# The channel weight's load issued in two pieces of partitions

## The chip, the cores and the metric

The kernel runs on one core of one Trainium2 chip. The metric is the device time of one execution in microseconds. All times of "before" are medians or single executions of the same program; a profile is one execution recorded by the hardware profiler.

## The reference

The input is q, k and v of shape (8, 8, 576, 64), two weight tensors w_r and w_i of shape (64, 512, 512), and a channel weight w_ch of shape (512, 512), all fp32. A causal attention with a window of 64 positions is followed by a spectral mix and a channel step:

```
scores = q @ k.T / sqrt(64);  masked to 0 <= i - j < 64
x      = softmax(scores) @ v                 -> (8, 576, 512)
X      = rfft(x, axis=1)[:, :64]             64 modes, complex
Y[m]   = X[m] @ (w_r[m] + i w_i[m])          one complex 512 x 512 product per mode
u      = x + irfft(Y, n=576)
out    = u + relu(u @ w_ch)                  fp32
```

The mode weights are the bulk of the input: 127 matrices of 1 MB are read (w_i of mode 0 isn't needed). w_ch is one matrix of 1 MB.

## The kernel before

**Attention.** For each of the 8 batches k, q and v are loaded (one DMA each, converted to bf16 on the way), transposed on TensorE, and worked through in windows of 512 score columns. The result x stays in SBUF in bf16 (`x_sb`). A forward transform on TensorE (`trigF`) makes the modes' inputs `XQ`.

**Modes.** The function `mode(m)` multiplies `XQ` with the two weight tiles of mode m: 16 matmuls of 128x128 by 128x16 per tile (line 563), summed into PSUM (`psy`). Eight modes share one PSUM tile, which `keep_y` copies into `YT` or `YTl`. The modes from 60 on go through `last_mode` (line 757) in a written order with idle matmuls (lines 721 and 723) between them.

**Weights.** Every weight is one DMA of 128 partitions, issued from GpSimd (POOL) by `load_w` (line 115): in the source each partition reads 8 KB of fp32 in one run and writes 4 KB of bf16. A tile's buffer is used again as soon as its mode is done: `mode` calls `refill_w`, which issues the next load. The DMAs of POOL use eight completion semaphores in turn, so a load is issued only when the load eight places before it has landed.

**The channel weight.** Inside the loop over the modes, after mode 6, one more DMA from POOL (line 608) fills `wch`, a tile of [128, 4, 512] in fp32r: partition p holds rows p, 128 + p, 256 + p and 384 + p of w_ch, four runs of 2 KB. It is read first by `channel` (line 594), which from mode 17 on computes x @ w_ch for each tile of x, and later by `turned` (line 706), which computes Y @ w_ch.

**End.** After the last weight the remaining rows of the modes' outputs are turned; small parts of them move from SBUF to SBUF (`send`, line 845: `yw<-yl` and `Yb<-yl`, 8 partitions of 2 KB each). Then `rectify` and `finish` compute the inverse transform, the relu and the sum, and the output is stored.

**Order.** TensorE's order is written by hand in the stretches under `manual_schedule`; elsewhere a scheduler orders each engine's instructions, and POOL's DMAs in the loop over the modes are among them.

Of the kernel before, what the change touches and what calls it, by code (L numbers as in the profile page):

```python
# [20 lines left out]
def view(ap, off, dims):  # L21

    return bass.AP(ap.tensor, ap.offset + off, [list(ap.ap[0])] + [list(d) for d in dims])
# [3 lines left out]
def kernel(  # L27
# [10 lines left out]
    nc = tc.nc  # L38
# [136 lines left out]
    for i in range(4):  # L175
        half = i % 2
        pp = slice(64 * (i // 2), 64 * (i // 2) + 64)
# [78 lines left out]
    for half in range(2):  # L256
        pp = slice(64 * half, 64 * half + 64)
# [233 lines left out]
    wch = late.tile([128, NC, DM], FP32R, name="wch")  # L491
# [80 lines left out]
    with ExitStack() as p2a:  # L572
# [28 lines left out]
        for m in range(L0 * MG):  # L601
            mode(m)
            if m == 8:
                for b in range(1, B, 2):
                    tc.keep_in_program_order(nc.scalar.copy(out=x_sb[64:128, b - 1, NT - 1, :],
                                                            in_=x_sb[64:128, b, NT - 1, :]))
            if m == 6:
                nc.gpsimd.dma_start(out=wch, in_=moe_w_ch.rearrange("(c p) e -> p c e", p=128))
            if m == Z_M:
                ps_t = p2a.enter_context(tc.tile_pool(name="ps_t", bufs=2, space=PSUM, reuse_waits="tile"))  # L610
                ps_z = p2a.enter_context(tc.tile_pool(name="ps_z", bufs=2, space=PSUM, reuse_waits="tile"))
# [219 lines left out]
    with tc.manual_schedule(engines={mybir.EngineType.PE, mybir.EngineType.Activation, mybir.EngineType.DVE,  # L831
                                     mybir.EngineType.Pool, mybir.EngineType.SP}):
        nc.vector.tensor_copy(out=view(YT2, R - RL, [[NR, NC], [R, 2], [1, RL]]),
                              in_=view(psl, 0, [[RL * B, NC], [RL, 2], [1, RL]]))
# [103 lines left out]
```

## Time and profile before

| | |
|---|---|
| median of 6 runs | 430.11 us (429.16 to 431.49) |
| the profiled execution's own time | 431.29 us |
| its span, first to last instruction | 429.5 us |
| mean granted TensorE clock | 0.797 |
| busy: PE, weight loads, DVE, ACT, POOL | 329.9, 234.2, 176.9, 164.3, 97.5 us |
| DMA | 92.17 MB written to the destinations, mean 215 GB/s |
| HBM read | 162.53 MB |
| issue to landing of a mode weight, median | 19.1 us |
| issue to landing of wch | 16.5 us |

The table's times are those of one profiled execution, except for the first row. A DMA of POOL counts as busy on POOL while its descriptors are made; the transfer itself runs later on the core's 16 DMA engines, and its landing is the last of 16 completion marks. GB/s counts bytes as they are written, so that a weight that is converted from fp32 to bf16 counts half of what was read.

### The profile page before, as it was taken

To read this page: it belongs to the slowest core of one execution; us is meant where nothing else is said; L and a number is where in the kernel's file an instruction comes from. 1 tells how busy PE (TensorE), PEld (TensorE's weight loads), DVE (VectorE), ACT (ScalarE), POOL (GpSimd) and SP (SyncE) were. 2 spreads that over 40 slices of the span, in tenths; PEclk is the share of its full clock that TensorE was granted. 3 is DMA by queue.
4 is the path that set the end of the run, shared out by engine and by line. 5 is a ranking of instruction groups with operands and counts; after the bars stand their busy time and mean duration, and the time that the engine had idled before them with its cause. 6 is when DMAs were issued, how large, how long until landed. Compare 5 with 4: busy or idle time off the path is not lost.

```text
span 429.5 us, 11626 instructions
## 1 busy us (share of the span) xinstructions
PE 329.9 (77%) x5186; PEld 234.2 (55%) x5186; DVE 176.9 (41%) x372; ACT 164.3 (38%) x290; POOL 97.5 (23%) x187
## 2 busy tenths in 40 slices
PE   6989999999998986422498797896367785498992
PEld 5755765665665476411376575664244552366681
DVE  5566764666764300306333342331113332141893
ACT  4585765676774211201031232222113221131991
POOL 7131231232012141212122121121111132100610
PEclk9999996899996565555588898887557866599998
DMA  7999999999999999999999999999999999993797
GB/s 141 212 214 212 212 214 213 209 213 213 213 204 193 212 210 260 214 213 214 213 214 214 213 213 214 214 213 214 214 213 214 214 213 213 214 214 69 237 365 298
DMA packets 28882, 92.17 MB, mean 215 GB/s; under 512 B 3136, under 2 KB 3392, under 8 KB 28832
## 3 DMA queue, kind: packets, MB, share of 16 engines
q0 software_dynamic: 25920, 82.52, 96.6%
q1 hardware_dynamic: 2768, 8.78, 5.4%
q8 instruction: 40, 0.66, 0.5%
q10 hardware_dynamic: 144, 0.13, 0.1%
q14 instruction: 10, 0.08, 0.0%
HBM read 162.53 MB, written 9.44 MB: 400 GB/s over the span
## 4 chain that ended last, share of the span: by engine, by line
DMA 44%; PE 35%; issue 9%; DVE 7%; ACT 2%; POOL 0%; DVEq 0%; POOLq 0%
DMA wt<-in_moe_w_r_dram 26%; DMA wt<-in_moe_w_i_dram 18%; PE pso L316 7%; PE pst L218 6%; PE psy L563 4%; PE psv L235 3%; PE psx L338 3%; DVE x_sb L324 3%; PE pso L856 3%; PE pss L372 3%; PE pss L272 2%; PE pss L291 2%; DVE vT L59 2%; ACT vt L58 1%; DVE ot L879 1%
## 5 line engine op out<-in xcount | busy, mean ns | idle before, releaser
L563 PE MATMUL psy<-XQ,wt 128*128 128x16 bf16 x1616 | 61.0, 191 | 67.6 <-DMA wt<-in_moe_w_i_dram 32.5
L563 PEld LDWEIGHTS <-wt 128*128 128x128 bf16 x1616 | 53.0, 104 | 83.0 <-DMA wt<-in_moe_w_i_dram 37.9
L591 DVE CAST xT<-pxt 128x256 fp32r<-128x256 bf16 (+1 forms) x68 | 26.5, 435 | 59.7 <-PE pxt L584 38.0
L115 POOL DMA_DIRECT2D wt<-in_moe_w_r_dram x54 | 29.0, 536 | 89.2 <-DMA wt<-in_moe_w_r_dram 39.6
L594 PE MATMUL psz<-wch,xT 128*128 128x512 f32 x144 | 47.5, 475 | 0.0
L596 ACT CAST Z<-psz 128x512 fp32r<-128x512 f32 x36 | 21.1, 586 | 66.4 <-PE psz L594 65.3
L115 POOL DMA_DIRECT2D wt<-in_moe_w_i_dram x52 | 27.9, 536 | 79.9 <-DMA wt<-in_moe_w_i_dram 46.4
L297 ACT ACTIVATE et<-pss 128x512 bf16<-128x512 f32 x72 | 39.2, 600 | 13.8 <-PE pss L291 13.8
L316 PE MATMUL pso<-vt,et 128*64 128x65 bf16 (+1 forms) x576 | 35.1, 213 | 4.8 <-DVE x_sb L324 4.7
L316 PEld LDWEIGHTS <-et 128*64 128x64 bf16 (+1 forms) x576 | 24.5, 117 | 17.5 <-issue 10.0
L594 PEld LDWEIGHTS psz<-wch,xT 128*128 128x128 f32 x144 | 30.1, 224 | 6.2 <-ACT Z L596 0.3
L324 DVE TENSOR_TENSOR x_sb<-pso,rcp 128x640 bf16<-128x640 f32 x32 | 26.3, 823 | 0.9
L59 DVE CAST YT<-psy 128x256 fp32r<-128x256 f32 x6 | 2.5, 425 | 50.7 <-PE psy L563 50.7
L879 DVE TENSOR_TENSOR ot<-pso,x_sb 128x512 f32<-128x512 f32 x35 | 22.3, 685 | 1.8 <-PE pso L856 1.5
L59 DVE CAST x_sb<-psj 128x512 bf16<-128x512 f32 x16 | 11.0, 689 | 27.0 <-PE psj L768 26.9
L272 PE MATMUL pss<-band,ident_bf 64*64 64x512 bf16 x136 | 20.9, 428 | 1.5 <-ACT et L297 1.5
L58 ACT CAST YT<-psy 128x256 fp32r<-128x256 f32 x6 | 2.2, 373 | 51.7 <-DVE YT L59 51.7
L59 DVE COPY vT<-pst 128x768 bf16<-128x768 bf16 x16 | 15.3, 958 | 14.6 <-PE pst L218 14.6
L58 ACT CAST x_sb<-psj 128x512 bf16<-128x512 f32 x16 | 9.4, 586 | 25.9 <-PE psj L768 25.9
L861 ACT ACTIVATE pso<-pso 128x512 f32<-128x512 f32 x36 | 19.2, 588 | 0.3 <-PE pso L856 0.2
L291 PE MATMUL pss<-qT,kT 64*64 64x128 bf16 (+1 forms) x640 | 17.8, 225 | 0.2 <-issue 0.2
L58 ACT COPY qT<-pst 128x768 bf16<-128x768 bf16 x16 | 12.9, 814 | 7.8 <-PE pst L218 7.6
(163 smaller groups left out, 526.6 us busy)
## 6 DMA issues: line engine op xcount, KB each, us to landing
wt<-in_moe_w_r_dram POOLq DMA_DIRECT2D x54, 512.0 KB, 19.1
wt<-in_moe_w_i_dram POOLq DMA_DIRECT2D x52, 512.0 KB, 19.1
out_dram<-ot SPq DMA_DIRECT2D x15, 512.0 KB, 5.3
rk<-in_k_dram POOLq DMA_DIRECT2D x8, 576.0 KB, 8.7
rq<-in_q_dram POOLq DMA_DIRECT2D x8, 576.0 KB, 11.9
rv<-in_v_dram POOLq DMA_DIRECT2D x8, 576.0 KB, 10.9
wy<-in_moe_w_r_dram POOLq DMA_DIRECT2D x3, 512.0 KB, 17.4
wy<-in_moe_w_i_dram POOLq DMA_DIRECT2D x3, 512.0 KB, 19.1
```

The costliest lines, as they stand in the source:

```text
L58: return nc.scalar.copy(out=o, in_=i)
L59: return nc.vector.tensor_copy(out=o, in_=i)
L115: nc.gpsimd.dma_start(out=wt, in_=src[m].rearrange("(p c) e -> p c e", c=NC))
L272: nc.tensor.matmul(out=pss[(2 * w + hh) % 3][64 * half:64 * half + 64, :], lhsT=ident_bf[pp, pp], rhs=view(band[pp], 128 * half, [[0, WIN ...
L291: nc.tensor.matmul(out=pss[(2 * w + hh) % 3][64 * half:64 * half + 64, col:col + nq], lhsT=kTs[b % 2][pp, g, 64 * kb:64 * kb + 64], rhs=qT ...
L297: nc.scalar.activation(out=et[:, hh, :], in_=pss[(2 * w + hh) % 3], func=ACT_F.Exp, scale=EX_SCALE)
L316: nc.tensor.matmul(out=pso[po, hh, (i // 2) * VW:(i // 2) * VW + D + 1], lhsT=et[pk, hh, col:col + 64], rhs=vt[pk, 1 - f % 2, 2 * hh + g / ...
L324: nc.vector.tensor_tensor(out=view(x_sb, b * NT * DM + g * D, [[4 * D, 2], [DM, NT], [1, D]]), in0=view(pso, 0, [[512, 2], [VW, NT], [1, D]]),
L563: nc.tensor.matmul(out=psy[:, m % MG, e, :], lhsT=w[:, c, 128 * e:128 * e + 128], rhs=XQ[:, c, :, 1 - im:3 - im, m], start=(m % MG == im + ...
L591: nc.vector.tensor_copy(out=xT[:, :, w * k:w * k + w], in_=view(psts[k], j, [[128, NC], [n, w]]))
L594: nc.tensor.matmul(out=psz, lhsT=xT[:, c, :], rhs=wch[:, c, :], start=(c == 0), stop=(c == NC - 1))
L879: nc.vector.tensor_tensor(out=ot[:, j], in0=ps, in1=x_sb[:, b, t, :], op=ALU.add)
```

## The change

The load of `wch` is issued as two DMAs: partitions 0 to 7, and partitions 8 to 127. Each has the three dimensions partition, chunk (4) and column (512). The bytes are the same and lie in the same places afterwards.

```diff
             if m == 6:
-                nc.gpsimd.dma_start(out=wch, in_=moe_w_ch.rearrange("(c p) e -> p c e", p=128))
+                for pp in (slice(0, 8), slice(8, 128)):
+                    nc.gpsimd.dma_start(out=wch[pp], in_=moe_w_ch.rearrange("(c p) e -> p c e", p=128)[pp])
```

In the built program the orders of PE, DVE, ACT and SP are the same as before. On POOL the piece of 8 partitions stands where the whole load stood, two mode weights follow it, and then comes the piece of 120 partitions.

## The prediction

> **What bounds the kernel now.** I read the page's slices and queue table first. The 16 DMA engines are busy from the second slice to the last weight, at one rate.
>
> ```profile
> span 429.5 us, 11626 instructions
> ...
> DMA  7999999999999999999999999999999999993797
> GB/s 141 212 214 212 212 214 213 209 213 213 213 204 193 212 210 260 214 213 214 213 214 214 213 213 214 214 213 214 214 213 214 214 213 213 214 214 69 237 365 298
> ...
> q0 software_dynamic: 25920, 82.52, 96.6%
> ...
> q8 instruction: 40, 0.66, 0.5%
> ```
>
> The digits are 9 in slices 2 to 36, and the rate is about 213 GB/s of bytes written, of bf16 out of fp32: twice that is read. Only the slice of the channel weight (260) stands out, since that load writes fp32. Next, the order of PE at the end of that stretch, to see who waits for the last bytes:
>
> ```profile
> 390.41 0.63 PE L757 MATMUL psl<-XQ,wy 128*128 128x16 bf16 x16 [0.42 <-DMA wy<-in_moe_w_r_dram]
> 390.87 1.10 PE L721 MATMUL psd<-Z,ident_r 128*128 128x512 f32 x2
> 391.81 0.66 PE L723 MATMUL psd<-x_sb,ident_bf 128*128 128x48 bf16 x20
> 392.85 0.65 PE L757 MATMUL psl<-XQ,wy 128*128 128x16 bf16 x16 [0.38 <-DMA wy<-in_moe_w_i_dram]
> 393.33 0.66 PE L723 MATMUL psd<-x_sb,ident_bf 128*128 128x48 bf16 x20
> 394.17 1.15 PE L706 MATMUL psw<-wch,YT 128*112 128x512 f32 x4 [0.17 <-DVE YT L835]
> ```
>
> PE fills in with idle matmuls and then waits for each weight. The last one releases it at 392.85; the tail that follows takes 429.5 - 392.85 = 36.7 us. So a microsecond on the last landing is a microsecond of the kernel. Then POOL's queue around the edit:
>
> ```profile
> 155.49 0.75 POOL L608 DMA_DIRECT2D wch<-in_moe_w_ch_dram  x1 [0.63 <-PE psy L563]
> 156.23 0.54 POOL L115 DMA_DIRECT2D wt<-in_moe_w_i_dram  x1
> 159.09 0.53 POOL L115 DMA_DIRECT2D wt<-in_moe_w_r_dram  x1 [2.32 <-PE psy L563]
> 160.01 0.53 POOL L115 DMA_DIRECT2D wt<-in_moe_w_i_dram  x1 [0.40 <-PE psy L563]
> 162.85 0.53 POOL L115 DMA_DIRECT2D wt<-in_moe_w_r_dram  x1 [2.31 <-DMA wt<-in_moe_w_i_dram]
> ```
>
> and the view of the tile:
>
> ```profile
> L594 PE MATMUL psz<-wch,xT x144: 388/399/776, 212.7 to 297.8; 128*128 128x512 f32 x144
> ...
> DMA to landing us min/median/max: 16.5/16.5/16.5
> ```
>
> The load is issued at 155.49, lands at 172.0, and its first reader starts at 212.7.
>
> **Which DMA engine is late.** Every transfer leaves 16 completion marks in the trace, one per DMA engine. At wch's landing they come 0 to 0.33 us after the first for ten engines, then at 0.68, 1.00, 1.09, 1.24, 1.87 and 2.00. At the last weight eight are within 0.75 us, and the others at 2.34, 2.91, 3.10, 3.14, 3.37, 3.44, 4.06 and 4.12: the last mark is at 392.81, the first at 388.69. The steps come with the 40 instruction packets (16 KB, 0.89 to 1.09 us each): the packet at 297.29 puts the last engine from 3.03 to 4.03 us behind. At 2.45 us a weight the latest engine has never run dry. Its sum of work is the end of the stream; the others have spare time, two excepted, the one at 4.06 (0.06 us) and with more room that at 3.44.
>
> **The change, part by part.** One POOL issue becomes two. In the built program's order the scheduler puts the 8-row piece where the load was, then two weights, then the 120-row piece. Nothing else moves but two weights and three iotas by one place.
>
> Issue: one more POOL instruction of 0.5 (a small copy's row, yw<-yl, 0.50) to 0.75 us. POOL then waits up to 2.3 us for a buffer or a landing, so it costs nothing; uncovered, 0.75 us. The weights wait for the landing of the transfer eight places earlier, so for one turn the eight in flight hold seven large ones: 7 x 2.45 = 17.2 us deep instead of 19.6, against 4.1 us of lag. No engine runs dry: nothing. The 120 rows land about two weights later, near 177; the reader at 212.7 has 35 us: nothing.
>
> What is left is how the bytes fall on the engines. Of the 512 wch packets (2,048 B) an engine has 32, one per 79 ns: 2.53 us and 26 GB/s written. A weight packet is 4,096 B per 305 ns: 13.4 GB/s written.
>
> The 120-row piece can't give eight rows to each of 16 engines. If rows stay whole, it gives eight to 15 and leaves one out, or 7 or 8 to all. The late engine then gets 2.2 to 2.5 us of it as before, or none. The 8-row piece has the yw<-yl copies of the tail (8 rows of 2,048 B) as its nearest row: the eight packets of the first start within 0.11 us and overlap, so they run on eight engines. wch's rows have four packets each: four more on eight engines, 4 x 79 ns = 0.32 us undisturbed.
>
> Disturbed is the word. Those eight packets, all written into eight partitions, take 106 to 412 ns, mean 192, where 98 is the commonest of such copies: 1.96 times as long. In the 128-row wch load 464 of 512 packets take 99 ns: there each engine must write partitions where no other is in its way. A 120-row copy starting at partition 8 need not keep that division. If it doesn't, an engine that wants 26 GB/s meets one that writes weights at 13.4 or another wch share in the same place. Bounds for the late engine's share: +0 (division kept) to the yl row's 1.96 x 2.53 - 2.53 = +2.4 us. Going below nothing needs the late engine to be the one left out, and the second, 0.06 us ahead, ends that. I take +2.4, the end nearest to the only row with an irregular partition range. The small piece: 0 if the late engine isn't among its eight, 0.3 undisturbed, 4 x 192 ns = 0.8 disturbed; I take 0.
>
> [...]
>
> Sum: 431.29 us (this execution's own time, span 429.5 and 1.8 around it) + 2.4 + 0 = 433.7. It is 1.18 above the median of the runs, 430.11, to which I forecast: 430.11 + 2.4 = 432.5.
>
> **Rivals.** *Absorbed.* The 120 rows keep the packets' rate. Then the late engine's sum changes by 0 to +0.3 us, or by -0.06 if it is left out: 430.05 to 430.4. For it: packets of the 128-row copy show no disturbance, and 13 of 16 engines have over 0.7 us to spare. Against it: the yl row.
>
> *Relief, not slower.* The engine left out is the late one, and in other executions it is late alone. The gain is min(2.5, its lead over the next): 0.06 us here, 0.7 where the second lacks its last fetch (4.12 - 3.44), 428.8 only if five engines are less late than here. Faster by over 1.3 us thus needs lags that this profile doesn't have.
>
> *It doesn't do what it says.* Were the 120-row piece late enough to hold the channel matmuls, the point is 35 us; it is two weights, 4.9.
>
> **How the numbers follow.** Disturbed 0.56, absorbed 0.32, relief or something not seen 0.12. 0.3% (1.3 us) is about what a measurement of this kernel can tell from no change; the forecast's +2.4 is past it, absorbed is within it. Disturbed has a range of its own: from +1.3 (half the yl row's price) to 2.4 + 0.8 = +3.2, plus 0.6 for the spread of the runs: 431.4 to 433.9. The whole range goes down to the absorbed case less 0.3: 429.7 to 433.9, leaving out most of relief and a worse disturbance.
>
> **What would show it.** Right: packets of 2,048 B near 170 to 180 us well over 99 ns, the late engine's mark 2 us later against the weights' 2.45 us pace after the 120 rows, the last wy landing near 395 and an unchanged tail of 36.7 us. Wrong: wch packets still at 99 ns; the lags at the last weight as before; or a first weight matmul that waits on POOL.

## The result, and the profile after

| | before | after |
|---|---|---|
| median | 429.90 us of 47 runs (429.02 to 432.24) | 432.17 us of 21 runs (431.01 to 435.50) |
| ratio after / before | | 1.0054, 95% interval 1.0042 to 1.0066 |
| the profiled execution's own time | 431.29 us | 431.33 us |
| its last landing of a mode weight (`wy`) | 392.81 us | 393.12 us |

The change costs 2.3 us (0.0054 x 429.9; by the interval 1.8 to 2.8). The two profiled executions are equally long all the same, so their spans must not be set against each other before it is seen why. The page after:

```profile
span 429.5 us, 11626 instructions
...
DMA  7999999999999999999999999999999999993797
GB/s 141 212 215 210 214 214 211 213 212 213 214 214 213 214 214 220 221 214 214 212 213 213 214 214 214 213 213 214 213 214 214 212 213 214 214 211 67 232 367 300
...
q0 software_dynamic: 26000, 82.52, 97.0%
...
q8 instruction: 40, 0.66, 0.6%
```

Two places differ from the row of before. In slices 12 and 13 (each slice is 429.5 / 40 = 10.74 us) before showed 204 and 193 GB/s where now 214 and 213 stand: 30 GB/s less for 10.74 us is 0.32 MB, or 1.5 us of a stream of 213 GB/s. The completion marks say the same: two weights before the channel weight the last of the 16 engines was at 166.84 us in before's profile and is at 165.17 us in this one. Before's profile had lost 1.67 us ahead of the changed lines. The stream of loads had run dry there. In before's profile the granted clock is 0.87 from 60 to 100 us, in after's 1.00; POOL issues the load that waits for the same transposes on TensorE at 119.00 us, in after's profile at 114.42; and in before's row from 115 to 145 us (0.75 us a slice) two slices, at 130.75 and 132.25 us, aren't full:

```profile
DMA  9999999999999999999996979999999999999999
```

The bytes fall to between 109 and 137 GB/s from 130.75 to 133 us, and the mean of the 16 marks loses 1.6 us over two loads. In after's row of this stretch every digit is 9. That the lower clock made the issues late is read from these numbers; no run varied it.

The second place is the load itself: slice 16 showed 260, now two slices show 220 and 221. The page counts bytes at their destination, and the same 1 MB of fp32 now goes in at nearly the pace of the bf16 weights.

POOL's queue around the edit stands as the built order had it, first the 8-row piece, two weights, then the 120-row piece:

```profile
151.32 0.58 POOL L609 DMA_DIRECT2D wch<-in_moe_w_ch_dram  x1 [2.23 <-DMA qT<-in_moe_w_i_dram]
153.18 0.56 POOL L115 DMA_DIRECT2D wt<-in_moe_w_i_dram  x1 [1.28 <-DMA vt<-in_moe_w_r_dram]
155.95 0.53 POOL L115 DMA_DIRECT2D wt<-in_moe_w_r_dram  x1 [2.21 <-DMA vt<-in_moe_w_i_dram]
158.14 0.82 POOL L609 DMA_DIRECT2D wch<-in_moe_w_ch_dram  x1 [1.67 <-DMA wt<-in_moe_w_r_dram]
```

Every one of these issues still ends an idle time of 1.3 to 2.2 us, so the extra issue is hidden. The view of the tile:

```profile
L594 PE MATMUL psz<-wch,xT x144: 387/399/776, 213.0 to 298.3; 128*128 128x512 f32 x144
...
DMA to landing us min/median/max: 17.3/18.7/20.1
```

The second piece lands at 158.14 + 20.1 = 178.2 us, 35 us before its first reader. The end of the weights in TensorE's order:

```profile
390.69 0.67 PE L758 MATMUL psl<-XQ,wy 128*128 128x16 bf16 x16 [0.35 <-DMA wy<-in_moe_w_r_dram]
391.20 1.10 PE L722 MATMUL psd<-Z,ident_r 128*128 128x512 f32 x2
392.15 0.66 PE L724 MATMUL psd<-x_sb,ident_bf 128*128 128x48 bf16 x20
393.16 0.65 PE L758 MATMUL psl<-XQ,wy 128*128 128x16 bf16 x16 [0.36 <-DMA wy<-in_moe_w_i_dram]
```

PE still waits for each weight, and from 393.16 to the end of the span are 36.3 us (36.7 before).

**Where the time goes.** The bytes written from 160 to 185 us show it, in 40 slices of 0.625 us. Before:

```profile
GB/s 236 197 216 203 210 216 216 210 210 216 223 252 338 390 400 361 292 239 233 210 236 197 210 210 210 216 210 210 210 223 216 216 203 216 216 216 216 210 216 223
```

After:

```profile
GB/s 249 197 210 210 210 210 233 220 216 216 223 216 203 216 226 259 226 226 223 272 259 216 203 213 239 210 203 210 223 210 216 210 216 216 210 223 216 210 223 203
```

Before, the channel weight shows as a hump of up to 400 GB/s from 167 to 171 us: its fp32 rows go in nearly twice as fast as the weights' bf16 rows (213 GB/s), from about the same read rate (1 MB in 2.69 us, a weight's 1 MB in 2.45). After, the hump is gone. The packet records give the reason. Of the 512 packets of 2,048 B of `wch`, before's take 99 ns in the median, 488 of them at most 105 ns, and 51.3 us in sum. After, 132 are at most 105 ns, the median is 214.5 ns, and the sum is 98.4 us. In completion marks (mean of the 16 engines): before, the load takes 2.69 us; after, the 8-row piece takes 0.45 us and the 120-row piece 4.55 us.

### The profile page after: what moved, and what is told of

It reads as the page before. It is cut to its first block, busy times and chain, and to the rows that moved or that the text cites. A ratio compares the mean times of both kernels' runs of the same rounds, so it can differ in the third digit from the quotient of the medians.

```text
span 429.5 us, 11626 instructions
## 1 busy us (share of the span) xinstructions
PE 321.3 (75%) x5186; PEld 229.6 (53%) x5186; DVE 176.5 (41%) x372; ACT 164.3 (38%) x290; POOL 98.2 (23%) x188
## 4 chain that ended last, share of the span: by engine, by line
DMA 48%; PE 32%; issue 8%; DVE 7%; ACT 1%; POOL 1%; DVEq 0%; POOLq 0%
DMA wt<-in_moe_w_r_dram 25%; DMA wt<-in_moe_w_i_dram 23%; PE pso L316 6%; PE pst L218 6%; PE psv L235 3%; DVE x_sb L324 3%; PE pso L857 3%; PE pss L372 2%; PE pss L272 2%; PE psx L338 2%; PE pss L291 2%; DVE vT L59 2%; PE psz L594 1%; PE psy L563 1%; PE psw L707 1%
## 5 line engine op out<-in xcount | busy, mean ns | idle before, releaser
L316 PE MATMUL pso<-vt,et 128*64 128x65 bf16 (+1 forms) x576 | 34.0, 209 | 5.2 <-DVE x_sb L324 5.1
L316 PEld LDWEIGHTS <-et 128*64 128x64 bf16 (+1 forms) x576 | 23.8, 114 | 17.2 <-issue 9.8
L291 PE MATMUL pss<-qT,kT 64*64 64x128 bf16 (+1 forms) x640 | 16.9, 219 | 0.1
L769 PE MATMUL psj<-x_sb,ident_bf 128*64 128x512 bf16 x64 | 14.4, 541 | 2.3 <-DVE x_sb L59 2.3
```

The lines of the kernel that those rows point to most:

```text
L291: nc.tensor.matmul(out=pss[(2 * w + hh) % 3][64 * half:64 * half + 64, col:col + nq], lhsT=kTs[b % 2][pp, g, 64 * kb:64 * kb + 64], rhs=qT ...
L316: nc.tensor.matmul(out=pso[po, hh, (i // 2) * VW:(i // 2) * VW + D + 1], lhsT=et[pk, hh, col:col + 64], rhs=vt[pk, 1 - f % 2, 2 * hh + g / ...
```

## The experiments

Each kernel is the kernel before with the edit shown; where only added lines stand, they replace the load of `wch` or, with `wt` in them, the issue in `load_w`. Times are medians beside runs of before in the same set. The ratio and its 95% interval are worked out from all runs, so that the ratio can differ a little from that of the two medians; a gain or loss in us is taken from it. "Undisturbed" is the number of `wch` packets that took at most 105 ns.

### The copy more, and the division of rows

**Two copies, all 128 partitions in each**

```diff
-                nc.gpsimd.dma_start(out=wch, in_=moe_w_ch.rearrange("(c p) e -> p c e", p=128))
+                for cc in (slice(0, 1), slice(1, 4)):
+                    nc.gpsimd.dma_start(out=wch[:, cc], in_=moe_w_ch.rearrange("(c p) e -> p c e", p=128)[:, cc])
```

> The channel weight still comes as two copies with two weights between them, but both have all 128 partitions (chunk 0, then chunks 1 to 3). Theory 'division lost' (a copy of fewer than 128 rows no longer gives each DMA engine partitions of its own, so that writes meet): no loss, the time of before within 0.5 us and nearly all 512 packets at 99 ns. Rival 'one more copy' (the extra issue on POOL and the extra place among the eight in flight cost the time): the change's loss again, +2.3 us.

Measured 429.88 us beside 430.20: ratio 0.9993 (0.9975 to 1.0012). All 512 packets are undisturbed, 50.7 us in sum, and the humps are back in the bytes from 160 to 185 us, one for each copy:

```profile
GB/s 229 210 210 210 229 203 229 259 252 206 236 226 275 229 203 236 298 315 282 239 259 311 298 292 197 216 210 210 210 223 203 216 216 216 229 203 210 216 229 216
```

A second copy costs nothing; its rows decide. This profile also is the better twin of after's, since it reaches the load at the same time (165.18 us two weights ahead, against 165.17). Its last `wy` lands at 391.19 us, after's at 393.12: 1.9 us between the two, which the profile of before hides. At 200 us it is already 1.8 us, so the loss arises at the load and stays.

**112 and 16 partitions**

```diff
+                for pp in (slice(0, 112), slice(112, 128)):
+                    nc.gpsimd.dma_start(out=wch[pp], in_=moe_w_ch.rearrange("(c p) e -> p c e", p=128)[pp])
```

> Rows 0 to 111, then 112 to 127: both counts divide by 16, so every engine can have seven rows of the one and one row of the other, 32 packets in all as in before. 'Division lost': the packets stretch to 200 ns and more as in the change, +1.5 to +3 us. Rival 'uneven count' (15 engines carry the 120 rows, eight of them carry the 8 rows as well, and the fullest sets the end): +0, since the counts are even.

Measured 431.85 us: 1.004 (1.0019 to 1.0061), so +1.7 us. 178 packets are undisturbed, 97.6 us in sum. The completion marks show no engine left out: the 112 rows move every one of the 16 on by 4 us or more (4.39 us in the mean). That a count such as 120 can't be shared evenly is not the cause.

**64 and 64 partitions**

```diff
+                for pp in (slice(0, 64), slice(64, 128)):
+                    nc.gpsimd.dma_start(out=wch[pp], in_=moe_w_ch.rearrange("(c p) e -> p c e", p=128)[pp])
```

> Rows 0 to 63, then 64 to 127: four rows of each on every engine. 'Division lost': all 16 engines write into half of the partitions at a time, +1.5 to +3 us, with packets at 200 ns in both copies. 'Uneven count' and 'one more copy': +0 and +2.3 us.

Measured 432.27 us: 1.0047 (1.0030 to 1.0064), +2.0 us. 166 undisturbed, 98.1 us in sum. Each half takes 2.62 and 2.75 us in the mean of the marks, as long as the whole `wch` before (2.69): an engine writes 12 GB/s (33 KB in 2.7 us), against 24 of the undivided load. Both of these even divisions of the rows lose about what the 8/120 one loses.

**A mode weight as 8 and 120 partitions, `wch` whole**

```diff
-        nc.gpsimd.dma_start(out=wt, in_=src[m].rearrange("(p c) e -> p c e", c=NC))
+        for pp in (slice(0, 8), slice(8, 128)) if i == 44 else (slice(0, 128),):
+            nc.gpsimd.dma_start(out=wt[pp], in_=src[m].rearrange("(p c) e -> p c e", c=NC)[pp])
```

> The channel weight is one copy again; instead one mode weight, the seventh after it, is issued as partitions 0 to 7 and 8 to 127. It reads as many bytes but writes bf16, 13.4 GB/s per engine instead of 26. 'Division lost' with a limit on writing into one place: two such writers fit where two of 26 did not, so that packets keep about 324 ns but for those that meet a third, +0 to +0.8 us. If the loss hangs on the rows alone and not on the rate of writing: packets of 600 ns, +2.3 us. 'Uneven count': +0.3 us.

Measured 430.21 us: 1.0009 (0.9989 to 1.0029). The rows are divided in the same way, and one engine is left out as in after (its mark at 182.18 us, the next at 184.32), but the packets of the copy (4,096 B, 182 to 188 us) keep their median of 324 ns; from 180 to 196 us 2 packets exceed 340 ns, as many as in after. Half the bytes are written per time, and by the time at most 1.2 us are lost, by the packets nothing. So neither the uneven share nor the rows of the copy alone double the packets. That it takes them together with what is written per us is the likeliest reading, but not shown: this load also reads 8 KB in one run where `wch` reads 2 KB. The engine left out brings no relief either.

### Which engine is left out, and which piece costs

**The 120 partitions first**

```diff
+                for pp in (slice(8, 128), slice(0, 8)):
+                    nc.gpsimd.dma_start(out=wch[pp], in_=moe_w_ch.rearrange("(c p) e -> p c e", p=128)[pp])
```

> The same two pieces of the channel weight in the other order: partitions 8 to 127, then 0 to 7. 'Division lost': the 120-row piece stretches its packets as before, +1.5 to +3 us. If it matters which engine is left out: in the change's trace it was one of the eight early engines; were it one of the eight late ones here, its relief of 2.5 us still leaves the next late one at most 0.1 us ahead, so the time is that of the change within 0.5 us under both.

Measured 433.22 us of 6 runs beside 430.18: 1.0063 (1.0040 to 1.0086). 134 undisturbed, 98.0 us in sum. One engine passes the 120 rows at 164.52, 4.25 us before the next (168.77); it is an early one again. Order doesn't matter.

**One chunk of four as 8 and 120 partitions**

```diff
+                src_ch = moe_w_ch.rearrange("(c p) e -> p c e", p=128)
+                for pp in (slice(0, 8), slice(8, 128)):
+                    nc.gpsimd.dma_start(out=wch[pp, 0:1], in_=src_ch[pp, 0:1])
+                nc.gpsimd.dma_start(out=wch[:, 1:4], in_=src_ch[:, 1:4])
```

> Only chunk 0 of the channel weight, a quarter of the bytes, comes as partitions 0 to 7 and 8 to 127; chunks 1 to 3 come as one copy of 128 partitions. 'Division lost': the loss goes with the bytes so copied, a quarter of 2.3 us: +0.3 to +0.9 us, with about 120 of the 512 packets stretched. Rival 'one more copy', with three copies now: +2.3 us or more.

Measured 430.52 us: 1.0003 (0.9988 to 1.0017), between -0.5 and +0.7 us. A loss in proportion, 0.6 us, isn't excluded by the time, nor by the last `wy` (391.56 us, 0.4 us after that of the two whole copies). But the packets did not do what was expected. 239 are undisturbed, and of the 273 others, more than twice the 120 expected, only 21 take over 150 ns. The sum is 57.8 us, 7.1 over the undisturbed 50.7, where the full split adds 47.7: a quarter of the rows' bytes brings 15% of the stretch. Why a short share gets off so lightly wasn't settled.

**Eight weights as 120 and 8 partitions, the order turned each time**

```diff
+        n, at = divmod(i - 50, 8)
+        pieces = [slice(0, 128)] if at or not 0 <= n < 8 else [slice(0, 8), slice(8, 128)][::1 if n % 2 != 0 else -1]
+        for pp in pieces:
+            nc.gpsimd.dma_start(out=wt[pp], in_=src[m].rearrange("(p c) e -> p c e", c=NC)[pp])
```

> The channel weight is one copy again. Eight mode weights, eight loads apart, come as 120 and 8 partitions, alternately with the 120 first and the 8 first. A 120-row copy of bf16 left one engine out and cost nothing. [...] If the engine left out is always the same one, or not a late one: 0 to +1.2 us.

The other way round (`n % 2 != 1`):

> The same eight mode weights in the opposite alternation, the 8 partitions first for the first of them. [...] If the place in the turn doesn't matter: the same time as the kernel with the other alternation, within 0.4 us.

Measured 432.23 us of 9 runs, 1.0049 (1.0031 to 1.0068), and 432.49 us of 7 runs, 1.0050 (1.0032 to 1.0067). Both lose 2.1 us; no gain, and no difference between the two. The first is a miss: a gain of 1.2 us had been hoped for, should the engine left out be another one at each split. In both kernels one and the same engine is left out every time. The marks carry no engine numbers, but at each of the eight splits it is the first mark that gains about 2 us on the others. Late in the row of splits its mark of one weight is at 309.45 us where the next engine's is at 317.43 and the last one's at 323.52; in the other kernel at 310.34, 319.74 and 324.52. At 14.1 us ahead it is about dry, by an estimate: a load isn't issued before the one eight places earlier has landed on all engines (in after's profile the load eight places behind the 120-row piece is issued at 178.77, 0.5 us after that piece's last mark), so that seven loads of 2.45 us, 17.2 us, are in flight then; this engine has 3.1 us of them left, the shortest time from POOL's issue to landing in before (`yw<-yl`). The late engine is never relieved. What is left for the 2.1 us, 0.26 us a split, is the 8-row pieces: their steps in the marks fall on a fixed set of eight engines, two of the late ones among them. At the last weight two engines end at 393.5 and 393.7 us in both kernels, 1.2 to 1.6 us after the next. That is read from the marks; no run varied it by itself.

### The 120 rows by themselves

**Only rows 8 to 127 are loaded** (rows 0 to 7 of `wch` are set to zero by VectorE; their part of the product is left out)

```diff
+                nc.vector.memset(wch[0:8].bitcast(FP32), 0.0)
+                nc.gpsimd.dma_start(out=wch[8:128], in_=moe_w_ch.rearrange("(c p) e -> p c e", p=128)[8:128])
```

> The 120-row piece without the 8-row piece: partitions 0 to 7 of the channel weight are set to zero by a small memset instead of being loaded, so the output differs from the reference in that part. 'Division lost' puts nearly all of the change's loss on the 120 rows: +1.5 to +2.5 us, packets of about 210 ns. Rival 'the small piece' (eight more rows on eight engines that already carry a full share): +0 to +0.4 us.

Measured 432.45 us of 6 runs beside 429.68: 1.0058 (1.0036 to 1.0080), +2.5 us. The copy of fewer bytes is the slower one: of 480 packets 105 are undisturbed, the sum is 100.4 us. The bytes from 160 to 185 us have no hump:

```profile
GB/s 210 223 236 197 210 210 226 252 233 220 220 233 292 233 197 216 210 193 190 200 197 203 210 210 229 203 210 216 210 210 216 210 216 210 216 216 223 223 216 216
```

and the last weight is as late as in after, or later:

```profile
394.14 0.65 PE L758 MATMUL psl<-XQ,wy 128*128 128x16 bf16 x16 [0.37 <-DMA wy<-in_moe_w_i_dram]
```

The 120 rows alone bring as much as both pieces, +2.5 us (1.5 to 3.4) beside +2.3 us (1.8 to 2.8). So the 8-row piece is worth about nothing, as it was taken, within the 1 us or so that the intervals leave.

**A mode weight as eight copies of 16 partitions**

```diff
+        n = 16 if i == 44 else 128
+        for p0 in range(0, 128, n):
+            pp = slice(p0, p0 + n)
+            nc.gpsimd.dma_start(out=wt[pp], in_=src[m].rearrange("(p c) e -> p c e", c=NC)[pp])
```

> The channel weight is one copy again; one mode weight (bf16, 13.4 GB/s per engine) comes as eight copies of 16 partitions, so that all 16 engines write into 16 partitions at a time, 214 GB/s in all. The halves of the channel weight took about 200 ns a packet instead of 99: 64 partitions take some 210 GB/s. 'In proportion to the rows' (16 partitions take a quarter of that, 52 GB/s): packets of 1,200 ns, +7 us and more. [...] If the rate into one place had no limit: +1 to +2 us for the copies alone.

Measured 432.19 us of 7 runs: 1.0067 (1.0042 to 1.0093), +2.9 us. But the packets of the copies mostly keep 324 ns; the time goes otherwise. The stretch from 176 to 196 us:

```profile
DMA  9999999999999976559643639289997989999999
GB/s 221 213 205 221 221 205 213 205 221 213 197 246 189 205 148 123 107 107 156 115 90 57 107 49 147 49 164 229 197 213 148 180 172 213 213 188 205 229 188 188
```

From 183 to 189 us (0.5 us a slice) the DMA engines stand partly idle; in before's row every digit of this stretch is 9. POOL's queue has the cause:

```profile
180.70 0.48 POOL L118 DMA_DIRECT2D wt<-in_moe_w_i_dram  x1 [1.97 <-DMA wt<-in_moe_w_r_dram]
184.04 0.48 POOL L118 DMA_DIRECT2D wt<-in_moe_w_i_dram  x1 [2.85 <-DMA wt<-in_moe_w_i_dram]
186.18 0.48 POOL L118 DMA_DIRECT2D wt<-in_moe_w_i_dram  x1 [1.66 <-DMA wt<-in_moe_w_r_dram]
186.76 0.55 POOL L118 DMA_DIRECT2D wt<-in_moe_w_r_dram  x1
187.37 0.14 POOL L622 IOTA pcol<- 128x1 f32 x1
187.45 0.24 POOL L627 IOTA pos<- 128x128 f32 x1
187.65 0.18 POOL L629 IOTA pos<- 128x64 f32 x1
187.78 0.56 POOL L118 DMA_DIRECT2D wt<-in_moe_w_i_dram  x1
```

Up to 186.18 every issue (0.48 us, the small ones) waits for the landing eight places before. With eight small copies filling the eight places, the engines have one weight of work in flight and use it up; from 186.76 on the large issues follow without a wait for a landing, into an empty queue. As a test of how few rows may be written into at once it decides less than hoped: the engines are two groups some 3 us apart, so only about eight were in one copy at a time. Only in the last of the eight copies do all 16 write at once (their marks lie within 0.30 us); its 16 packets start out of the emptied queue and take 322 to 554 ns, 404 in the mean. That is far from the 1,200 ns of 'in proportion to the rows', on one packet an engine.

**A mode weight as four copies of 32 partitions** (the same with `n = 32`)

> The same mode weight as four copies of 32 partitions. [...] 'In proportion to the rows': 105 GB/s, packets of 600 ns, +2.5 to +3.3 us.

Measured 430.67 us: 1.0027 (1.0007 to 1.0047), +1.2 us (0.3 to 2.0). The packets stay at 324 ns, not the 600 of 'in proportion to the rows', and the engines don't run dry, except for single digits of 8:

```profile
DMA  9989999999899998999999999999999899999998
```

The stream lost 0.1 us over this weight by the last marks (2.53 us against 2.45). Where the rest of the 1.2 us is stays open; the profiled execution has its last `wy` at 391.52 us and then a tail of 37.9 us.

**Four copies of one chunk, all 128 partitions in each**

```diff
+                for c in range(NC):
+                    nc.gpsimd.dma_start(out=wch[:, c], in_=moe_w_ch.rearrange("(c p) e -> p c e", p=128)[:, c])
```

> The channel weight as four copies of all 128 partitions, one chunk each: the price of three more copies by itself, as a control for the kernels that cut a weight into several copies. All theories of the rows: packets at 99 ns, +0 to +0.6 us (0.0 to 0.2 us a copy). 'One more copy' as the cause of the change's loss: +2 us and more.

Measured 430.19 us beside 429.68: 0.9999 (0.9983 to 1.0015), so at most +0.6 us. 511 of 512 packets are undisturbed, 50.8 us in sum. Three copies more cost nothing that shows either, as long as each has all 128 rows.

## Why the prediction was right

| the sum's terms | forecast | measured |
|---|---|---|
| packets of the 120 rows | 1.96 times as long | 1.92 times (98.4 / 51.3 us, both pieces) |
| late engine | +2.4 us | +1.9 us between twin profiles, +2.3 us (1.8 to 2.8) by the runs |
| 8-row piece | 0 (to 0.8) | about 0: 120 rows alone +2.5 us (1.5 to 3.4) |
| one more issue | 0 | 0: second copy -0.3 us (-1.1 to +0.5) |
| engine left out | relief 0.06 us at most | none |
| time | 432.5 us (429.7 to 433.9) | 432.17 us |

**What bounds it.** That the stream of weights sets the end, and that a microsecond on the late engine is about one of the kernel, held: the last `wy` moves, the tail stays between 35.9 and 37.4 us in all profiles but one (37.9). The loss arises at 172 to 178 us and is still there at 393, because from there on the late engine doesn't run dry: its marks follow each other every 2.46 us in the median, in both profiles. It has no idle time that could cover the loss; only the other engines have. Two readings of the time ahead of the load were wrong, without harm to the forecast: not only the slice of 260 GB/s stands out in before's row, but 204 and 193 too, and there the stream had run dry (the 16 marks close up from 3.18 to 1.22 us over two loads). That the latest engine never runs dry is shown only from then on.

**The division.** The step that carried the forecast was that a copy of 120 rows loses the division of partitions between engines. In the five kernels with the whole `wch` divided across partitions (the change, 112/16, 64/64, the order turned, 120 alone) its packets take 97.6 to 100.4 us in sum; in the others, with all 128 rows in each copy of `wch`, 50.7 to 51.8 us; the quarter lies between, with 57.8 us. That it is the engines' division of partitions that is lost remains the author's reading: no trace shows which rows an engine writes. The size was taken from a far row (eight packets of `yw<-yl`, mean 192 ns against 98), and that the ratio was met to 2% is more than the row could promise: that is luck. The likely rival, that the packets' rate is kept, falls with the packets at 214.5 ns. It is what the mode weight in 8 and 120 rows does: packets of 324 ns and no loss that shows.

**The engine left out.** The prediction left open whether 120 rows go to 15 engines or to all, and priced relief at 0.06 us for want of a lead. The marks show 15, with an early engine left out: its mark of the 120 rows is at 169.65 us, the next at 173.69, and its lead over the last goes from 3.75 to 8.59 us. That there is no relief was right by its number, but the reason is stronger: in the two kernels of eight splits it's the same engine every time, and not the late one.

**The signs named.** Packets well over 99 ns: yes. The late mark 2 us later: between the weights on both sides of the load the last mark goes from 1.67 us ahead of before's to 0.90 us behind it, 2.57 us, of which a part is an instruction packet that fell there in one profile and later in the other. The last `wy` near 395: no, it landed at 393.12, because that number was built on a profile that had lost 1.67 us ahead of the load, and the next execution hadn't. The forecast itself was made to the median and so did not carry this over.

**What isn't shown.** Where the engines meet: that they get in each other's way at the same partitions, or in writing at all. The packets show that a copy of `wch` without all 128 rows is half as fast (99 ns become 214.5), and that the bf16 copy at 13.4 GB/s written an engine is not slowed (324 ns stay 324). No run changed the place written or the rate alone, and the reading differs too: runs of 2 KB against 8 KB. That 64 partitions take some 210 GB/s, as was worked out from the packets of 200 ns before the copies of 16 and 32 rows were run, the half loads don't confirm: their engines come to the first half one after another, from 164 to 170 us, and the packets of `wch` wrote at most 184 GB/s in any half microsecond, mostly under 110, and were still twice as long. What other loads wrote to the same partitions meanwhile can't be told from the trace.

## What to carry to other kernels

Where a stream of loads bounds the kernel as here, divide a load along its free dimension and keep all 128 partitions in each copy: one, two or four such copies cost the same (at most 0.6 us more), and each division of the whole fp32 load across partitions cost 1.7 to 2.7 us for its 1 MB. Look at the DMA packets of one size, not only at the page: the engines are as busy as before (queue 0's packets 97.0% against 96.6%), and only the bytes per us in the stretch tell. And before two profiled spans are compared, compare their marks ahead of the edit: here a lag of 1.67 us in one of them hid nearly the whole loss.

## What the runs showed that was not expected

- The same 8/120 division of a 1 MB load costs 2.3 us where it writes fp32 (26 GB/s per engine, 99 ns become 214.5), and no time that shows where it is converted to bf16 (13.4 GB/s, 324 ns stay 324). The rate of writing is the likeliest reason; the length of the runs read wasn't ruled out.
- A copy of fewer rows was slower than one of all: 480 packets took 100.4 us, 512 took 51.3.
- A copy of 120 rows leaves out the same engine at all eight splits of a kernel, whether the 8 rows go before or behind it; eight of them put this engine up to 14 us ahead, which helps nobody. The three-dimensional copies of `wch` leave out an early engine too; whether it is the same one the marks can't tell.
- Eight copies in flight were a limit on bytes too: eight copies of 16 rows hold 0.5 MB together where eight whole weights hold 4 MB, and the engines ran out of work; it cost 2.9 us.
